# Layer 1's GpSimd subtraction in two halves, and seven VectorE steps of a weight conversion spread over four tiles

## The chip, the cores and the metric

The kernel runs on one core of one Trainium2 chip. The metric is the device time of one execution in microseconds; the time before is the median of three runs. TensorE does the matrix products, VectorE, ScalarE and GpSimd the elementwise work, SyncE (SP) and GpSimd issue transfers.

## The reference

A two-dimensional Fourier transform (real part) of four sequences of 3008 rows and 256 columns, followed by two feed-forward layers over the 12032 rows. The weights are float64.

```python
def reference(x, moe_w_in, moe_w_out, moe2_w_in, moe2_w_out):
    X = np.fft.fft(np.fft.fft(x, axis=1), axis=2).real.astype(np.float32)
    X = X.reshape(4 * 3008, 256)
    h = X @ moe_w_in                      # 256 x 2048
    X = (np.maximum(h, 0.0) ** 2) @ moe_w_out      # 2048 x 256
    h = X @ moe2_w_in
    return ((h * np.cos(h)) @ moe2_w_out).astype(np.float32)
```

## The kernel before

All products are done with operands split into two parts of 12 bits each (a high one, `h`, and a low one, `l`), so that each product is three matmuls: high by high, low by high, high by low. The transform along the rows is done with folded tables, the transform along the columns is multiplied into the first weights.

Layer 1 goes over 12 blocks of up to 512 pairs of tokens (the last has 388), and in each block over 16 tiles of 128 hidden columns: 192 tiles, numbered `i` from 0. A pair holds the sum and the difference of two halves, so that a tile is 128 by 2 by 512. The chain of one tile is:

- `l1_mm1`: TensorE, six matmuls into a PSUM buffer `h`, of which there are two; then `l1_add` on VectorE: `u` (line 450) and the two sums `s` (line 206 in the helper `tt`), which read `h` and so release it for the tile after the next.
- `l1_act` on ScalarE: three instructions of 128x1024, relu, square, and the high part `gh`.
- `l1_lo` on GpSimd (line 470): `gl = s - gh`, 128x1024.
- `l1_mm2`: TensorE, twelve matmuls into `acc`, three tiles later (`LAG`).

After 16 tiles `l1_out` takes `acc` out: two instructions on ScalarE, two of 128x1024 on VectorE (`ol`), stored by SP. Layer 2 follows in the same manner with 128x512 halves.

Each engine executes its instructions in the order in which the program issues them. That order comes from the class `Order`: each piece of work is given a time, in units of one tile, and all are issued in the order of these times. Work of tile `i` has the times `i` (`l1_mm1`), `i + 0.4` (`l1_add`), `i + 0.6`, `i + 0.8` and `i + 3.3`; a table `TIMES` holds other times for much of the work before tile 107, and is the same in both kernels.

The weights come as float64 and are converted by `from_f64` in steps on VectorE, with `size_f64` on ScalarE ahead of them. For layer 1's weights this lies in tiles 0 to 18, with some steps handed to ScalarE and GpSimd (`shared`). For layer 2's weights there are 16 pieces of 128x512, one for every four tiles from 113 on: piece `p` is loaded by SP at time 111 + 4p (`load_cv`), sized on ScalarE at 113 + 4p, and converted by `conv_w2` at 113.5 + 4p: seven VectorE instructions one behind the other (lines 164, 165, 166, 171, 175, 176, 178), then two stores to DRAM. The converted weights are read back from tile 181 on. The folds of batches 1 to 3 (`fold_a`, `fold_eo`, `fold_b`, `fold_lo`) are VectorE work of the same kind, spread over tiles 11 to 24, 36 to 48 and 84 to 96.

Of the kernel before, what the change touches and what calls it, by code (L numbers as in the profile page):

```python
# [10 lines left out]
F32 = mybir.dt.float32  # L11
F32R = mybir.dt.float32r
I32 = mybir.dt.int32
# [29 lines left out]
# the upper half of float64's least value that float32 holds too, read as float32  # L43
SMALLEST = float(np.array([0x38100000], np.int32).view(np.float32)[0])

# columns of the transforms' tables, one for each part
# [6 lines left out]
# of each part of a transform, by columns of the result: (column, width, ((unit of the data, column of the table), ..))  # L53
# [6 lines left out]
# of each tile of rows: (sum over even or over odd places, rows)  # L60
# [3 lines left out]
# the places in the order of issue of instructions that do not have the one they get by rule; what converts with help from other engines; which engine folds  # L64
# [5 lines left out]
class Order:  # L70
    """Instructions gathered with a time each and issued in the order of those times."""
# [13 lines left out]
def f32(ap):  # L85
    return ap.bitcast(F32)
# [3 lines left out]
def kernel(ctx: ExitStack, tc: tile.TileContext, x, x128, cs, tab0, tab1, w_in1, w_out1, w_in2, w_out2, out):  # L90
# [36 lines left out]
    # a chunk of a layer's weights holds four tiles of d_ff, as two parts of 12 bits each  # L127
# [26 lines left out]
    def from_f64(key, st, hi, lo, pool=fft, shared=False):  # L154
        """float64 as the sum of two float32r: the first holds 12 bits, the second the rest, rounded to 12 bits."""
        n = st.shape[1]
        w0, w1 = st[:, :, 0], st[:, :, 1]
        r = w1.bitcast(F32)
        v = nc.vector
        got = {}  # L160

        def upper():
            a = got["a"] = buf("f64t", "f64t", I32, pool, 2, (P, BLK))[:, :n]
            v.tensor_scalar(out=a, in0=w1, scalar1=0x07FFFE00, scalar2=3, op0=ALU.bitwise_and, op1=ALU.logical_shift_left)  # L164
            v.scalar_tensor_tensor(out=a, in0=w1, scalar=-0x40000000, in1=a, op0=ALU.bitwise_and, op1=ALU.bitwise_or)  # L165
            v.tensor_scalar(out=w1, in0=w1, scalar1=0x1FF, scalar2=None, op0=ALU.bitwise_and)
            if shared:
                nc.scalar.activation(r, w1, AF.Copy, scale=2.0 ** -20)
                nc.gpsimd.tensor_tensor(out=r, in0=w0.bitcast(F32), in1=r, op=ALU.add)
            else:  # L170
                v.scalar_tensor_tensor(out=r, in0=w0.bitcast(U32), scalar=2.0 ** -32, in1=w1, op0=ALU.mult, op1=ALU.add)

        def parts():
            a = got["a"]
            v.scalar_tensor_tensor(out=hi, in0=sizes.pop(key), scalar=SMALLEST, in1=a.bitcast(F32), op0=ALU.is_ge, op1=ALU.mult)  # L175
            v.tensor_scalar(out=a, in0=hi.bitcast(I32), scalar1=-0x800000, scalar2=None, op0=ALU.bitwise_and)  # L176
            if not shared:
                v.scalar_tensor_tensor(out=lo, in0=r, scalar=2.0 ** -20, in1=a.bitcast(F32), op0=ALU.mult, op1=ALU.mult)

        def lower():  # L180
            if shared:
                nc.gpsimd.tensor_tensor(out=lo, in0=r, in1=got["a"].bitcast(F32), op=ALU.mult)

        return upper, parts, lower

# [38 lines left out]
    def fold_b(b, t):  # L224
        ra, rb = raws[b, t]
        eo = units(rb, "p (e a d) -> p e a d", e=2, a=4)
        # units: cosE s s', sinO s s', cosO s s', sinE s s'
        f = units(ra, "p (i a b d) -> p i a b d", i=2, a=2, b=2)
        for i, op in enumerate(PM):
            tt(f[:, i], eo[:, :, 0::2], eo[:, :, 1::2], op)  # L230
        # units: eeC, eoS, eoC, eeS
        fv = units(ra, "p (a b d) -> p a b d", a=4, b=2)
        g = units(rb, "p (i a d) -> p i a d", i=4, a=2)
        for i, op in enumerate(PM):
            tt(g[:, i], fv[:, 0:4:3, 0], fv[:, 0:4:3, 1], op)

    def fold_hi(b, t):
        ra, rb = raws[b, t]
        # units: sinO s s', cosO s s', eeC, eoS, eoC, eeS
        src = (units(ra, "p (a n) -> p a n", a=4)[:, 1:3], units(rb, "p (a n) -> p a n", a=4)[:, 0:2])  # L240
        parts = [buf(f"d{p}", f"d{p}", F32R, fft, NT, (P, 2, 2, 2 * P)) for p in "hl"]
        for i in range(2):
            nc.scalar.activation(parts[0][:, i], src[i], AF.Copy)
        raws[b, t] = src, parts
# [11 lines left out]
    def fold_128():  # L256
# [5 lines left out]
        # units: cosO s s', eeC, eoC  # L262
# [28 lines left out]
    def both(s, n, a, m):  # L291
        """The sums over even and over odd places, added and subtracted."""
        for i in (1, 0):
            tt(s[:m, i, :n], s[:m, 0, :n], a[:m, 1, :n], PM[i])
# [94 lines left out]
    def conv_w2(name, c, q):  # L389
        parts = [buf(f"cv{p}", f"cv{p}", F32R, late["pool"], 2, (P, BLK)) for p in "hl"]  # L390
        for fn in from_f64((name, c, q), wst.pop((name, c, q)), *parts, late["pool"]):
            fn()
        for p, dst in zip(parts, w2_dram[name, c]):
            nc.sync.dma_start(out=dst[:, q * BLK:(q + 1) * BLK], in_=f32(p))
# [28 lines left out]
    def direct_z(i, s, hi, lo):  # L423
        """The first block's columns stay on the chip; the rest of the sums s goes to DRAM."""
# [41 lines left out]
    def l1_lo(k, f):  # L466
        w = BLOCKS[k][1]
        hi, s = gs[1, k, f], ss.pop((k, f))
        lo = gl_buf()
        nc.gpsimd.tensor_tensor(out=lo[:, :, :w], in0=s[:, :, :w], in1=f32(hi)[:, :, :w], op=ALU.subtract)  # L470
        gs[1, k, f] = hi, lo
# [129 lines left out]
    def convert(t, key, st, fn, steps=(-0.5, 0, 0, 0)):  # L601
# [3 lines left out]
        def start():  # L605
            got.extend(fn(shared))
            got[0]()

        at(t + steps[0], lambda: size_f64(key, st(), shared=shared), ("size", key))
        for i, f in enumerate((start, lambda: got[1](), lambda: got[2]())):  # L610
            at(t + steps[1 + i], f, ("conv", key, i))
# [96 lines left out]
    for i, job in enumerate((n, c, q) for n in ("in", "out") for c in range(NCH) for q in range(2)):  # L708
        at(111 + 4 * i, lambda job=job: load_cv(*job))
        at(113 + 4 * i, lambda job=job: size_f64(job, wst[job], late["pool"]))  # L710
        at(113.5 + 4 * i, lambda job=job: conv_w2(*job))
# [28 lines left out]
def _order():  # L740
    """The place along s of each row of the folded data, or -1: even ones, odd ones, the last of both."""
# [12 lines left out]
def _tables():  # L754
    """The transforms' cosines and sines, in two parts of 12 bits each."""
# [15 lines left out]
# the places along d, the first half of them; the last row of the sines holds the place in the middle  # L771
# [10 lines left out]
def _rows():  # L782
    """For each of the eight places that fold onto s its row of x, or S where there is none."""
# [9 lines left out]
def _lay_x(x):  # L793
    """x with rows and columns in the order in which they are folded, zeros where nothing folds; the middle column."""
# [16 lines left out]
def _token_columns():  # L811
    """The column of the result in which each token lies."""
# [38 lines left out]
```

## Time and profile before

| | us |
|---|---|
| median of three runs | 2033.5 (2033.21 to 2036.59) |
| span of the profiled execution, first to last instruction | 2030.6 |
| TensorE busy (matmuls) | 1915.8, 94% of the span |
| VectorE busy | 1439.9, 71% |
| ScalarE busy | 1470.2, 72% |
| GpSimd busy | 1043.5, 51% |

The median lies 2.9 us above the span of the profiled execution. The page cuts the span into 40 slices of 50.8 us. From the fifth on TensorE is busy for nine tenths or more, except in three of eight tenths between 711 and 965 us, and from the fourth on its granted clock is at nine tenths or more. In the slices from 608 to 914 us VectorE's share rises to between seven and eight tenths; after about 990 us layer 2 runs, and the slices are alike.

### The profile page before, as it was taken

To read this page: it belongs to the slowest core of one execution; us is meant where nothing else is said; L and a number is where in the kernel's file an instruction comes from. 1 tells how busy PE (TensorE), PEld (TensorE's weight loads), DVE (VectorE), ACT (ScalarE), POOL (GpSimd) and SP (SyncE) were. 2 spreads that over 40 slices of the span, in tenths; PEclk is the share of its full clock that TensorE was granted. 3 is DMA by queue.
4 is the path that set the end of the run, shared out by engine and by line. 5 is a ranking of instruction groups with operands and counts; after the bars stand their busy time and mean duration, and the time that the engine had idled before them with its cause. 6 is when DMAs were issued, how large, how long until landed. Compare 5 with 4: busy or idle time off the path is not lost.

```text
span 2030.6 us, 23279 instructions
## 1 busy us (share of the span) xinstructions
PE 1915.8 (94%) x8544; PEld 1587.5 (78%) x8544; DVE 1439.9 (71%) x1558; ACT 1470.2 (72%) x1519; POOL 1043.5 (51%) x524
## 2 busy tenths in 40 slices
PE   5678999999999988998999999999999999999999
PEld 4466877887787776777888888888888888888899
DVE  8999576457847878887576666666666666666666
ACT  3666777787767767667787777777777777777776
POOL 5455655564555645555554444544444544444443
PEclk8789999999999999999999999999999999999999
DMA  6222231212222233223611111111111111111110
GB/s 245 91 89 83 87 111 69 80 61 90 83 85 101 68 109 104 88 89 113 192 52 32 32 31 32 53 42 32 31 32 32 52 43 31 32 32 32 51 33 16
DMA packets 64389, 140.17 MB, mean 69 GB/s; under 512 B 7680, under 2 KB 19088, under 8 KB 64276
## 3 DMA queue, kind: packets, MB, share of 16 engines
q1 hardware_dynamic: 41524, 89.20, 12.4%
q0 software_dynamic: 22752, 49.49, 8.4%
q8 instruction: 67, 1.10, 0.2%
q14 instruction: 46, 0.38, 0.1%
HBM read 81.98 MB, written 56.69 MB: 68 GB/s over the span
## 4 chain that ended last, share of the span: by engine, by line
PE 75%; DVE 18%; issue 2%; ACT 2%; DMA 2%; POOL 1%; DVEq 0%; ACTq 0%; POOLq 0%; SPq 0%
PE acc L566 25%; PE h L515 17%; PE acc L482 15%; PE h L443 8%; PE acc L515 8%; DVE s L206 4%; DVE u L450 2%; DVE f64t L165 2%; PE h L281 2%; DVE inB L206 2%; DVE cvh L175 1%; DVE f64t L164 1%; DVE f64t L176 1%; DVE inA L206 1%; DMA ol<-ol 1%
## 5 line engine op out<-in xcount | busy, mean ns | idle before, releaser
L554 POOL TENSOR_TENSOR gl<-r,gh 128x1024 fp32r<-128x1024 f32 (+1 forms) x189 | 446.2, 2361 | 540.0 <-ACT gh L547 465.9
L470 POOL TENSOR_TENSOR gl<-s,gh 128x1024 fp32r<-128x1024 f32 (+1 forms) x192 | 466.5, 2430 | 353.1 <-ACT gh L463 311.3
L460 ACT ACTIVATE s<-s 128x1024 f32<-128x1024 f32 (+1 forms) x192 | 199.1, 1037 | 196.0 <-DVE s L206 188.6
L529 DVE SCALAR_TENSOR_TENSOR r<-n,h 128x1024 f32<-128x1024 int32 (+1 forms) x129 | 154.7, 1199 | 214.6 <-ACT n L521 214.6
L450 DVE SCALAR_TENSOR_TENSOR u<-zb,wc,h 128x512 f32<-128x512 f32 (+1 forms) x192 | 141.0, 734 | 178.9 <-PE h L443 174.4
L206 DVE TENSOR_TENSOR s<-u,h 128x512 f32<-128x512 f32 (+1 forms) x384 | 242.7, 674 | 24.5 <-POOL inB L319 2.6
L521 ACT ACTIVATE n<-h 128x1024 int32<-128x1024 f32 (+1 forms) x129 | 130.4, 1011 | 155.3 <-PE h L515 155.3
L482 PE MATMUL acc<-gh,wbh 128*128 128x512 f32 (+1 forms) x768 | 242.3, 398 | 0.0
L482 PE MATMUL acc<-gh,wbl 128*128 128x512 f32 (+1 forms) x768 | 238.8, 393 | 0.0
L482 PE MATMUL acc<-gl,wbh 128*128 128x512 f32 (+1 forms) x768 | 237.6, 391 | 0.0
L529 DVE SCALAR_TENSOR_TENSOR r<-n,r 128x1024 f32<-128x1024 int32 (+1 forms) x192 | 232.7, 1212 | 6.6
L443 PE MATMUL h<-xh,wah 128*128 128x512 f32 (+3 forms) x384 | 159.2, 415 | 71.8 <-DVE s L206 63.7
L537 ACT ACTIVATE r<-r,halfpi 128x1024 f32<-128x1024 f32 (+1 forms) x192 | 218.3, 1137 | 6.2
L461 ACT ACTIVATE s<-s 128x1024 f32<-128x1024 f32 (+1 forms) x192 | 200.5, 1044 | 6.1
L463 ACT ACTIVATE gh<-s 128x1024 fp32r<-128x1024 f32 (+1 forms) x192 | 200.5, 1044 | 6.1
L536 ACT ACTIVATE r<-r 128x1024 f32<-128x1024 f32 (+1 forms) x192 | 198.3, 1033 | 6.7 <-DVE r L529 6.7
L566 PE MATMUL acc<-gh,wbl 128*128 128x512 f32 (+1 forms) x768 | 202.2, 385 | 0.0
L566 PE MATMUL acc<-gh,wbh 128*128 128x512 f32 (+1 forms) x768 | 202.1, 385 | 0.0
L566 PE MATMUL acc<-gl,wbh 128*128 128x512 f32 (+1 forms) x768 | 202.1, 385 | 0.0
L515 PE MATMUL h<-xh,wah 128*128 128x512 f32 (+1 forms) x516 | 199.0, 386 | 3.0 <-issue 1.5
L515 PE MATMUL h<-xh,wal 128*128 128x512 f32 (+1 forms) x516 | 198.8, 385 | 0.0
L515 PE MATMUL h<-xl,wah 128*128 128x512 f32 (+1 forms) x516 | 198.8, 385 | 0.0
(160 smaller groups left out, 3513.9 us busy)
## 6 DMA issues: line engine op xcount, KB each, us to landing
oh<-oh SPq DMA_DIRECT2D x22, 512.0 KB, 2.9
ol<-ol SPq DMA_DIRECT2D x22, 512.0 KB, 2.7
xh<-oh POOLq DMA_DIRECT2D x22, 512.0 KB, 3.9
xl<-ol POOLq DMA_DIRECT2D x22, 512.0 KB, 5.0
y_out<-o SPq DMA_DIRECT2D x44, 256.0 KB, 3.9
inA<-x_in SPq DMA_DIRECT2D x12, 512.0 KB, 3.9
inB<-x_in SPq DMA_DIRECT2D x10, 512.0 KB, 5.9
xh<-zh POOLq DMA_DIRECT2D x10, 512.0 KB, 4.1
```

What stands on the lines that cost most here:

```text
L206: nc.vector.tensor_tensor(out=out, in0=in0, in1=in1, op=op)
L443: nc.tensor.matmul(a[:, i, :w], st, mv[:m, i, :w], start=j == 0, stop=j == 2)
L460: nc.scalar.activation(s[:, :, :w], s[:, :, :w], AF.Relu)
L461: nc.scalar.activation(s[:, :, :w], s[:, :, :w], AF.Square)
L463: nc.scalar.activation(hi[:, :, :w], s[:, :, :w], AF.Copy)
L470: nc.gpsimd.tensor_tensor(out=lo[:, :, :w], in0=s[:, :, :w], in1=f32(hi)[:, :, :w], op=ALU.subtract)
L482: nc.tensor.matmul(accs[1, k][m][:, n, :w], wt, g[:, n, :w], start=f == 0 and i == 0, stop=f == NF - 1 and i == 2)
L515: nc.tensor.matmul(a[:, j, :w], st, mv[:, m, :w], start=m == 0 and q == 0, stop=m == 1 and q == 2)
L529: nc.vector.scalar_tensor_tensor(out=r[:, :, :w], in0=n[:, :, :w], scalar=-c, in1=src[:, :, :w], op0=ALU.mult, op1=ALU.add)
L537: nc.scalar.activation(r[:, :, :w], r[:, :, :w], AF.Sin, bias=halfpi, scale=-1.0)
L554: e.tensor_tensor(out=lo[:, :, :w], in0=r[:, :, :w], in1=f32(hi)[:, :, :w], op=ALU.subtract)
L566: nc.tensor.matmul(accs[2, k][:, m, :w], w_out_t([c[part] for c in wo2], f, m), g[:, j, :w], start=f == 0 and q == 0, stop=f == NF - 1 and ...
```

## The change

Two edits. `l1_lo` subtracts in two instructions of 128x512 in place of one of 128x1024. And `from_f64` returns seven functions of one VectorE step each in place of three; `convert`, which serves layer 1's weights, calls them in the groups that stood there before, and `conv_w2` gives them times of their own, 4/7 of a tile apart, with the stores at 3.9 tiles behind the first step. The other lines of the difference are comments that fell away.

```diff
     def from_f64(key, st, hi, lo, pool=fft, shared=False):
...
-        def upper():
+        def mask():
             a = got["a"] = buf("f64t", "f64t", I32, pool, 2, (P, BLK))[:, :n]
             v.tensor_scalar(out=a, in0=w1, scalar1=0x07FFFE00, scalar2=3, op0=ALU.bitwise_and, op1=ALU.logical_shift_left)
-            v.scalar_tensor_tensor(out=a, in0=w1, scalar=-0x40000000, in1=a, op0=ALU.bitwise_and, op1=ALU.bitwise_or)
+
+        def merge():
+            v.scalar_tensor_tensor(out=got["a"], in0=w1, scalar=-0x40000000, in1=got["a"], op0=ALU.bitwise_and, op1=ALU.bitwise_or)
+
+        def rest():
             v.tensor_scalar(out=w1, in0=w1, scalar1=0x1FF, scalar2=None, op0=ALU.bitwise_and)
+
+        def join():
             if shared:
...
-        def parts():
+        def upper_part():
...
+        def power():
...
-        def lower():
+        def lower_part():
...
-        return upper, parts, lower
+        return mask, merge, rest, join, upper_part, power, lower_part
...
-    def conv_w2(name, c, q):
-        parts = [buf(f"cv{p}", f"cv{p}", F32R, late["pool"], 2, (P, BLK)) for p in "hl"]
-        for fn in from_f64((name, c, q), wst.pop((name, c, q)), *parts, late["pool"]):
-            fn()
-        for p, dst in zip(parts, w2_dram[name, c]):
-            nc.sync.dma_start(out=dst[:, q * BLK:(q + 1) * BLK], in_=f32(p))
+    def conv_w2(t, name, c, q):
+
+        got = {}
+
+        def begin():
+            got["p"] = [buf(f"cv{p}", f"cv{p}", F32R, late["pool"], 2, (P, BLK)) for p in "hl"]
+            got["f"] = from_f64((name, c, q), wst.pop((name, c, q)), *got["p"], late["pool"])
+
+        def store():
+            for p, dst in zip(got["p"], w2_dram[name, c]):
+                nc.sync.dma_start(out=dst[:, q * BLK:(q + 1) * BLK], in_=f32(p))
+
+        at(t, begin)
+        for j in range(7):
+            at(t + 4 / 7 * j, lambda j=j: got["f"][j]())
+        at(t + 3.9, store)
...
         lo = gl_buf()
-        nc.gpsimd.tensor_tensor(out=lo[:, :, :w], in0=s[:, :, :w], in1=f32(hi)[:, :, :w], op=ALU.subtract)
+        for n in range(2):
+            nc.gpsimd.tensor_tensor(out=lo[:, n, :w], in0=s[:, n, :w], in1=f32(hi)[:, n, :w], op=ALU.subtract)
...
-        at(113.5 + 4 * i, lambda job=job: conv_w2(*job))
+        conv_w2(113.5 + 4 * i, *job)
```

VectorE's row at the second piece, of the kernel before. `u` and `s` are a tile's additions, `f` is the loaded piece, `f64t`, `cvh` and `cvl` are the conversion's results:

```order
L450 SCALAR_TENSOR_TENSOR u_4956<-zb,wc_96,h 128x512
L206 TENSOR_TENSOR s<-u_4956,h 128x512 x2
L164 TENSOR_SCALAR f64t<-f_4878 128x512
L165 SCALAR_TENSOR_TENSOR f64t<-f_4878,f64t 128x512
L166 TENSOR_SCALAR f_4878<-f_4878 128x512
L171 SCALAR_TENSOR_TENSOR f_4878<-f_4878 128x512
L175 SCALAR_TENSOR_TENSOR cvh<-size,f64t 128x512
L176 TENSOR_SCALAR f64t<-cvh 128x512
L178 SCALAR_TENSOR_TENSOR cvl<-f_4878,f64t 128x512
L450 SCALAR_TENSOR_TENSOR u_4998<-zb,wc_96,h 128x512
L206 TENSOR_TENSOR s<-u_4998,h 128x512 x2
```

VectorE's row at the same piece, of the kernel after; its lines 469 and 215 are 450 and 206 of before, and 164 to 190 the seven steps:

```order
L215 TENSOR_TENSOR s<-u_5071,h 128x512 x2
L164 TENSOR_SCALAR f64t<-f_4987 128x512
L167 SCALAR_TENSOR_TENSOR f64t<-f_4987,f64t 128x512
L469 SCALAR_TENSOR_TENSOR u_5109<-zb,wc_96,h 128x512
L215 TENSOR_TENSOR s<-u_5109,h 128x512 x2
L170 TENSOR_SCALAR f_4987<-f_4987 128x512
L177 SCALAR_TENSOR_TENSOR f_4987<-f_4987 128x512
L469 SCALAR_TENSOR_TENSOR u_5144<-zb,wc_96,h 128x512
L215 TENSOR_TENSOR s<-u_5144,h 128x512 x2
L180 SCALAR_TENSOR_TENSOR cvh<-size,f64t 128x512
L183 TENSOR_SCALAR f64t<-cvh 128x512
L469 SCALAR_TENSOR_TENSOR u_5177<-zb,wc_96,h 128x512
```

Seven steps between two tiles' additions became two, two, two and one, the last behind the fourth tile's additions; the next piece begins one tile later in the same way.

GpSimd's row early in layer 1, before and then after (`gl` is the subtraction, `inB` and `wo` are steps of layer 1's weights):

```order
L470 TENSOR_TENSOR gl<-s,gh 128x1024
L319 TENSOR_TENSOR zl<-z,zh 128x2x378
L470 TENSOR_TENSOR gl<-s,gh 128x1024
L169 TENSOR_TENSOR inB_488<-inB_488 128x512
L470 TENSOR_TENSOR gl<-s,gh 128x1024
```

```order
L490 TENSOR_TENSOR gl<-s,gh 128x512 x2
L328 TENSOR_TENSOR zl<-z,zh 128x2x378
L490 TENSOR_TENSOR gl<-s,gh 128x512 x2
L175 TENSOR_TENSOR inB_489<-inB_489 128x512
L490 TENSOR_TENSOR gl<-s,gh 128x512 x2
```

Each subtraction is now two instructions in the same place, and nothing else on GpSimd moved. On SP a piece's two stores moved behind the load of the next piece, and where a block ends behind the four stores of its results; the orders of TensorE and ScalarE are unchanged.

## Rows read from the trace of the kernel before

**Rows 1.** Busy time by stage, microseconds; the first line names the columns.

```profile
core 0: us, PE busy (x) PEld busy (x) DVE busy (x) ACT busy (x) POOL busy (x), PEclk, DMA share, GB/s
42.60:250.00 207.40, 170.42 (x746) 134.33 (x745) 177.03 (x226) 137.90 (x156) 117.32 (x62) 0.89 0.28 91
250.00:440.00 190.00, 184.49 (x832) 151.22 (x832) 121.02 (x162) 141.43 (x144) 109.17 (x49) 0.97 0.24 82
...
480.00:550.00 70.00, 64.27 (x265) 51.75 (x264) 61.33 (x72) 50.22 (x51) 38.55 (x17) 0.95 0.23 77
...
621.02:937.70 316.68, 278.28 (x1136) 223.47 (x1134) 260.50 (x306) 209.62 (x210) 163.59 (x71) 0.94 0.28 94
```

**Rows 2.** That last stage, first product (L443) alone, six matmuls a tile.

```profile
621.02:937.70 316.68, 105.68 (x379) 73.65 (x378) 0.94 0.28 94
```

**Rows 3.** Waits in 621 to 938 us: total, times, longest.

```profile
PE h L443 <- DVE s L206: 38.4, 14, 4.5
```

**Rows 4.** TensorE in order of time: start, us, instruction, [idle before].

```profile
621.02 0.39 PE L443 MATMUL h<-xh,wah 128*128 128x512 f32 x1
...
625.12 0.39 PE L443 MATMUL h<-xh,wah 128*128 128x512 f32 x1
...
695.73 0.50 PE L443 MATMUL h<-xh,wah 128*128 128x512 f32 x1 [1.81 <-DVE s L206]
...
698.05 1.06 PE L482 MATMUL acc<-gh,wbl 128*128 128x512 f32 x2
...
701.12 0.62 PE L482 MATMUL acc<-gl,wbh 128*128 128x512 f32 x2
```

**Rows 5.** Groups of VectorE's steps in 621 to 938 us, by line.

```profile
...
L166 DVE TENSOR_SCALAR f<-f 128x512 int32<-128x512 int32 x16 | 14.7, 920 | 1.9 <-ACT size L150 0.5
L171 DVE SCALAR_TENSOR_TENSOR f<-f 128x512 f32<-128x512 uint32 x16 | 13.2, 823 | 0.6
...
L206 DVE TENSOR_TENSOR ol<-acc,oh 128x1024 fp32r<-128x1024 f32 x8 | 9.4, 1216 | 0.0
```

**Rows 6.** VectorE's instructions on tile f64t: five of the seven steps.

```profile
621.02:937.70 316.68, 101.95 (x80) 0.00 (x0) 0.94 0.28 94
```

**Rows 7.** VectorE in order of time, sixth piece: first and last step.

```profile
728.89 0.47 DVE L164 TENSOR_SCALAR f64t<-f 128x512 int32<-128x512 int32 x1
...
733.05 0.74 DVE L450 SCALAR_TENSOR_TENSOR u<-zb,wc,h 128x512 f32<-128x512 f32 x1
```

**Rows 8.** VectorE in order of time, fourth piece and the tile behind it.

```profile
...
685.09 0.47 DVE L164 TENSOR_SCALAR f64t<-f 128x512 int32<-128x512 int32 x1
685.59 2.78 DVE L165 SCALAR_TENSOR_TENSOR f64t<-f,f64t 128x512 int32<-128x512 int32 x1
...
689.55 2.89 DVE L175 SCALAR_TENSOR_TENSOR cvh<-size,f64t 128x512 fp32r<-128x512 bf16 x1
...
693.54 0.74 DVE L450 SCALAR_TENSOR_TENSOR u<-zb,wc,h 128x512 f32<-128x512 f32 x1
694.39 1.29 DVE L206 TENSOR_TENSOR s<-u,h 128x512 f32<-128x512 f32 x2
```

**Rows 9.** GpSimd in order of time, around the fourth piece.

```profile
...
682.84 4.98 POOL L470 TENSOR_TENSOR gl<-s,gh 128x1024 fp32r<-128x1024 f32 x2
689.01 2.88 POOL L470 TENSOR_TENSOR gl<-s,gh 128x1024 fp32r<-128x1024 f32 x1 [1.19 <-DVE f L166]
...
```

**Rows 10.** VectorE's additions of tile 113.

```profile
623.45 1.28 DVE L206 TENSOR_TENSOR s<-u,h 128x512 f32<-128x512 f32 x2
```

**Rows 11.** GpSimd beside that addition.

```profile
624.11 2.41 POOL L470 TENSOR_TENSOR gl<-s,gh 128x1024 fp32r<-128x1024 f32 x1 [1.41 <-ACT gh L463]
```

**Rows 12.** All engines, tile 117: from VectorE's sums to GpSimd's subtraction.

```profile
645.87 1.29 DVE L206 TENSOR_TENSOR s<-u,h 128x512 f32<-128x512 f32 x2
...
650.64 2.65 POOL L470 TENSOR_TENSOR gl<-s,gh 128x1024 fp32r<-128x1024 f32 x1 [2.48 <-ACT gh L463]
```

**Rows 13.** Instructions on tile f64t: duration ns min/median/max, first and last start.

```profile
...
L182 POOL TENSOR_TENSOR wbl<-wo,f64t x7: 1290/1327/2159, 82.1 to 165.6; 128x512 fp32r<-128x512 f32 x7
...
```

More of the change, by code (lines that the diff above doesn't have):

```diff
@@ L171, in upper @@
                 v.scalar_tensor_tensor(out=r, in0=w0.bitcast(U32), scalar=2.0 ** -32, in1=w1, op0=ALU.mult, op1=ALU.add)
-        def parts():
[L174 to L178, printed above, removed]
-        def lower():
+        def upper_part():
+            v.scalar_tensor_tensor(out=hi, in0=sizes.pop(key), scalar=SMALLEST, in1=got["a"].bitcast(F32), op0=ALU.is_ge, op1=ALU.mult)
+        def power():
+            v.tensor_scalar(out=got["a"], in0=hi.bitcast(I32), scalar1=-0x800000, scalar2=None, op0=ALU.bitwise_and)
+        def lower_part():
+            a = got["a"].bitcast(F32)
             if shared:
-                nc.gpsimd.tensor_tensor(out=lo, in0=r, in1=got["a"].bitcast(F32), op=ALU.mult)
-        return upper, parts, lower
+                nc.gpsimd.tensor_tensor(out=lo, in0=r, in1=a, op=ALU.mult)
+            else:
+                v.scalar_tensor_tensor(out=lo, in0=r, scalar=2.0 ** -20, in1=a, op0=ALU.mult, op1=ALU.mult)
+        return mask, merge, rest, join, upper_part, power, lower_part
     raws, dat, jobs = {}, {}, {}
@@ L606, in start, with middle, last @@
             got.extend(fn(shared))
-            got[0]()
+            for g in got[:4]:
+                g()
+        def middle():
+            for g in got[4:6]:
+                g()
+            if not shared:
+                got[6]()
+        def last():
+            if shared:
+                got[6]()
         at(t + steps[0], lambda: size_f64(key, st(), shared=shared), ("size", key))
-        for i, f in enumerate((start, lambda: got[1](), lambda: got[2]())):
+        for i, f in enumerate((start, middle, last)):
             at(t + steps[1 + i], f, ("conv", key, i))
```

## The prediction

> **What bounds the kernel now.** I read the page's 40 slices first: TensorE is busy nearly throughout, but between 609 and 914 us its share and its granted clock dip while VectorE's share rises. Then the busy time by stage [rows 1]. From tile 113's first product at 621.02 us to tile 176's at 937.70 lie 63 tiles (378 weight loads by six a tile, [rows 2]) in 316.68 us. Undisturbed, one tile follows the other after 4.10 us (625.12 - 621.02, [rows 4]), so 63 tiles want 258.3 us: this stage loses 58.4 us. Two views account for it. TensorE is idle for 316.68 - 278.28 = 38.4 us, all of it waiting for VectorE's sums `s` [rows 1, 3]; and its granted clock is 0.94 on average, so that 0.06 x 316.68 = 19.0 us of cycles are missing. The clock is at its full level (2.4 GHz) before such a wait and at half of it (1.2 GHz) behind the longer ones: behind the wait that ends at 695.73, pairs of matmuls take 1.06 us, and 0.62 once the clock is back [rows 4]. The rest of the losses stand in the stages of the first weights and of the folds, where VectorE is nearly full or TensorE idles beside it [rows 1].
>
> Why `s` is late: the seven steps of a piece stand in one burst between two tiles' additions. Undisturbed, the burst takes 733.05 - 728.89 = 4.16 us [rows 7]. On average it takes (101.95 + 14.7 + 13.2) / 16 = 8.1 us [rows 5, 6]; the other 3.9 us are waits inside instructions. The fourth piece shows what for: GpSimd runs two subtractions back to back from 682.84, 4.98 us together. Line 164's step comes at 685.09, just as the first ends, and takes 0.47; line 165's comes at 685.59 and lasts 2.78 instead of some 0.69, until 688.37, which is 0.55 behind GpSimd's second end at 687.82 [rows 8, 9]. So a step and a subtraction take turns: whichever has begun keeps the other out to its end, and a step that waits gets in between two subtractions. The additions, which read PSUM, show no such wait.
>
> The burst is too long for the cover it has. Tile 113's sums end at 623.45 + 1.28 = 624.73 [rows 10]; TensorE wants that buffer for tile 115, at 621.02 + 8.20 = 629.22. VectorE may be 4.5 us late; a burst of 8.1 us less the idle VectorE had (4.10 - 2.24 = 1.9 a tile) is later than that.
>
> **The change part by part.** *The seven steps, spread.* Nothing is removed: 16 x 4.16 us of steps stay on VectorE. Additions take 0.74 + 1.29 and 0.11 between, so 2.14, or 2.24 from one to the next (rows 8: 693.54, 694.39). Four tiles of these (9.0), a piece (4.2) and a quarter of a block's two `ol` (9.4 / 16 = 0.6, [rows 5]) make 13.7 us of the 16.4 that TensorE needs for four tiles. That leaves 2.7 us for waits, and 4.5 us of lateness that may build up and be paid back.
>
> How long the waits are I walk through by hand. Time 0 is the end of the additions after which a piece begins. GpSimd starts 3.5 us behind the end of the sums it works on (645.87 + 1.29 to 650.64, [rows 12]; ScalarE's three instructions lie between). With tiles 4.10 apart, the previous tile's subtraction has started at -0.6, which is where 624.11 lies against 624.73 [rows 11]. A half of it: no row shows this form; 2.41 / 2 = 1.21 is the bound below, and 1.33, the median of another GpSimd operation of 128x512 with two inputs, the bound above [rows 13]. I take 1.26, between them, and 0.08 between two (4.98 - 2 x 2.41 over two, rounded up).
> - First tile: the first half ends at 0.6, the first step gets in and ends at 0.9; the second half ends at 2.1, the second step at 2.6. The additions end at 4.7, where 4.1 would be punctual: 0.6 late.
> - Second: the previous subtraction started at 3.5 and ends at 6.1; both steps are done by 7.1, the additions end at 9.2, 1.0 late.
> - Third: GpSimd starts at 8.2, the first half ends at 9.5; the step that waits ends at 10.0, the second half at 11.3, the next step at 11.6; the additions end at 13.7, 1.4 late.
> - Fourth, one step: the first half ends at 13.9, the step at 14.5, the additions at 16.6, 0.2 late. By now the next subtraction starts at 17.2, so the next piece's first two steps run free (16.6 to 17.8) and the additions are punctual again.
>
> The lateness stays at 1.4 us; with a block's two `ol` in the same tile (2 x 1.2 us more) at 3.8, still under 4.5. By this walk TensorE waits no more and its clock has no reason to fall. The margin is thin in the tiles where a block ends, and the walk is sensitive to a few tenths, so I leave 8 us of the 58.4 (half a microsecond a piece) and count 50 gained. What is late next is TensorE itself, at 4.10 us a tile.
>
> *The halves.* GpSimd does 192 x about 0.2 us more (2 x 1.26 + 0.08 - 2.41). It hides in GpSimd's idle time, since it is then busy for 2.6 of 4.1 us a tile, and `gl` is used three tiles later. Were that cover gone, it would cost 0.2 us a tile. In return a VectorE step with such a wait waits for at most one half. That matters also ahead of tile 113, in the first weights and the folds. There, from 250 to 440 and from 480 to 550 us, TensorE idles for 5.5 + 5.7 us and lacks 0.03 x 190 + 0.05 x 70 = 9.2 us of clock, and from 43 to 250 us VectorE is busy for 177 of 207 us [rows 1]. Where several steps stand in a row, the second half catches the next one, so little is saved. Bounds: -18 us (most of that 20) and +5 (GpSimd's 0.2 in each of some 25 tiles of the first stage). I take -5, nearer to nothing than to the end.
>
> *The rest.* SP's stores come later, each behind a wait for the last step; behind them in SP's queue stands the load of the next piece but one, whose first reader is two tiles (8.2 us) off, and the stored weights are read from tile 181 on, four tiles after the last store. I count nothing; had a load to wait for the store, ScalarE's size instruction would hold up its chain by as much. `convert` issues the same order as before.
>
> Sum, against the profiled execution's span: 2030.6 - 50 - 5 = 1975.6 us. The median lies 2.9 us above that span, so 1978.5.
>
> **A rule that speaks against it.** The rows show a step kept out to the end of a subtraction, and one subtraction held up by a step (2.88 us at 689.01 for 2.41, [rows 9]). The Trainium skill, SBUF — State Buffer, section "Who interferes with whom", says the same of the port pair that VectorE shares with GpSimd: an exclusive lock, held for a whole instruction, and taken also by a VectorE instruction with two inputs in SBUF. By that rule all seven steps are of the kind that waits, and the trace agrees (line 164 and line 165 both wait). It would make spreading a cost, since each step asks anew; that is the third rival below.
>
> **The rivals.**
> 1. *VectorE becomes the bound.* If a step does not get in between the two halves, the walk changes: the steps wait for the whole subtraction, 2.6 us, and only the fourth tile pays back. Additions then end at 5.1, 9.2, 14.3 and 18.0: 1.6 us late for each piece, plus 0.6 for `ol`; 16 x 2.2 less the 4.5 us of cover, which is there once, leaves 31 of the 58 us lost, and the halves bring nothing elsewhere: 2033.5 - 27 = 2006. For it: the gap between two subtractions is short. Against it: at 685.09 a step did get in. Chance 0.22.
> 2. *The halves do more than I count.* The folds and the first weights lose most of their waits: 18 us in place of 5, and the whole 58 us here: 2033.5 - 58 - 15 = 1960. For it: VectorE is the late engine there too. Against it: the steps stand in rows there. Chance 0.10.
> 3. *Slower: each step meets a half.* Seven waits of 1.26 us make 8.8 in place of 3.9, and a piece of four tiles 13.7 + 8.8 = 22.5 us of VectorE against the 316.68 x 4 / 63 = 20.1 of now: 16 x 2.4 = 38 us more, 2072. It decides from 6.4 us of waits a piece on (20.1 - 13.7), 0.9 a step. For it: GpSimd and VectorE's free time fall together in each tile. Against it: the walk finds 0.4 to 0.9 for the waiting ones, and some run free. Chance 0.05.
> 4. *Nothing to measure.* The change does what it says on VectorE, but TensorE's waits return elsewhere in the same sum, for instance on `gl`, whose subtraction now ends later: 2033. Against it: rows 3 and the cover of three tiles. Chance 0.03.
>
> **How the numbers follow.** Forecast 0.60, rivals 0.22, 0.10, 0.05, 0.03. The time is 1978. The range goes from 1960 (rival 2) to 2010 (rival 1 with the bound of +5): it leaves out rivals 3 and 4 and the outer parts of 1 and 2, some 0.17. Faster by over 0.2% (4 us, about what a measurement of this kernel can tell from no change): 0.92; within it 0.03; slower 0.05.
>
> **What would show it.** Right: from tile 113 to tile 176 some 266 us in place of 316.7, with a granted clock of 0.99 or more and under 10 us of TensorE's first product waiting for `s`; 384 subtractions of about 1.26 us; steps of a piece that last at most 1.3 us longer than their 0.4 to 0.7. Wrong: steps of 2 to 3 us still (the halves run as one), first products that wait a little in most tiles (rival 1), or ends of blocks with waits over 2 us, at which the clock falls to half again.

## The result and the profile after

The changed kernel takes 1971.7 us (median of four runs, 1970.0 to 1974.1) against 2033.4: 0.969 of the time before, with an interval of 0.968 to 0.971. The profiled execution's span fell from 2030.6 to 1968.2 us, by 62.4. It splits by TensorE's first products as before:

| | before | after | gain |
|---|---|---|---|
| start to tile 113's first product | 621.02 us | 614.32 us | 6.7 |
| tile 113's to tile 176's (63 tiles) | 316.68 | 259.65 | 57.0 |
| from there to the end | 1092.9 | 1094.2 | -1.3 |

The slices of the page: the dip of TensorE and of its clock around 609 to 914 us is gone, and VectorE's row reads nine where it read seven and eight.

```profile
PE   5688999999999999999999999999999999999999
...
DVE  8999587455947999995766666666666666666666
...
PEclk9789999999999999999999999999999999999999
```

Busy time by stage, as [rows 1]; the last line is the 63 tiles:

```profile
core 0: us, PE busy (x) PEld busy (x) DVE busy (x) ACT busy (x) POOL busy (x), PEclk, DMA share, GB/s
41.62:248.86 207.24, 174.20 (x747) 136.96 (x746) 176.95 (x228) 137.91 (x156) 128.38 (x94) 0.89 0.29 92
248.86:614.32 365.46, 355.52 (x1627) 291.83 (x1626) 235.52 (x318) 276.74 (x279) 234.01 (x179) 0.99 0.25 83
614.32:873.97 259.65, 259.10 (x1136) 212.87 (x1134) 246.75 (x303) 213.28 (x212) 182.23 (x134) 1.00 0.35 113
```

TensorE is now busy for 259.10 of 259.65 us with the clock at its full level; 63 tiles at 4.10 us are 258.3. VectorE is busy for 246.75 of them: it is nearly full, and does not hold TensorE up. The waits of that stage, where 38.4 us stood before [rows 3]:

```profile
...
DVE u L469 <- PE h L462: 1.9, 1, 1.9
...
PE h L462 <- DVE s L215: 0.3, 1, 0.3
...
```

TensorE's wait for `s` is 0.3 us in all. But the other line says as much: VectorE waited once, for 1.9 us, for a first product. In all other tiles it came to its additions after the product was there. So it is late all through the stage, and stays within the cover. What the stage still takes over 258.3 us lies where a block ends (tiles 132, 163 and 164, against the same tiles of a run without any loss, the quarters below).

VectorE in order of time, the sixth piece (164, 167, 170, 177, 180, 183 and 190 are the seven steps, 469 and 215 the additions):

```profile
...
702.39 0.42 DVE L164 TENSOR_SCALAR f64t<-f 128x512 int32<-128x512 int32 x1
702.85 0.69 DVE L167 SCALAR_TENSOR_TENSOR f64t<-f,f64t 128x512 int32<-128x512 int32 x1
703.46 0.74 DVE L469 SCALAR_TENSOR_TENSOR u<-zb,wc,h 128x512 f32<-128x512 f32 x1
704.33 1.29 DVE L215 TENSOR_TENSOR s<-u,h 128x512 f32<-128x512 f32 x2
705.53 0.72 DVE L170 TENSOR_SCALAR f<-f 128x512 int32<-128x512 int32 x1
706.29 0.69 DVE L177 SCALAR_TENSOR_TENSOR f<-f 128x512 f32<-128x512 uint32 x1
...
708.95 1.03 DVE L180 SCALAR_TENSOR_TENSOR cvh<-size,f64t 128x512 fp32r<-128x512 bf16 x1
710.01 1.57 DVE L183 TENSOR_SCALAR f64t<-cvh 128x512 int32<-128x512 int32 x1
...
713.58 1.41 DVE L190 SCALAR_TENSOR_TENSOR cvl<-f,f64t 128x512 fp32r<-128x512 f32 x1
...
```

GpSimd beside it, two halves a row:

```profile
...
703.15 2.82 POOL L490 TENSOR_TENSOR gl<-s,gh 128x512 fp32r<-128x512 f32 x2 [1.60 <-ACT gh L482]
706.87 2.56 POOL L490 TENSOR_TENSOR gl<-s,gh 128x512 fp32r<-128x512 f32 x2 [0.90 <-ACT gh L482]
710.01 2.74 POOL L490 TENSOR_TENSOR gl<-s,gh 128x512 fp32r<-128x512 f32 x2 [0.57 <-DVE cvh L180]
713.14 3.01 POOL L490 TENSOR_TENSOR gl<-s,gh 128x512 fp32r<-128x512 f32 x2 [0.40 <-PE acc L502]
...
```

The steps at 702.39 and 702.85 run free, others wait for one half: 708.95 lasts 1.03 us for 0.69, 710.01 lasts 1.57 for 0.43, 713.58 lasts 1.41 for 0.69. None lasts 2.8 us, as in [rows 8]; the longest of the stage lasts 1.82. This piece is one of the cheapest, 6.5 us of steps for 7.9 on average. The step of line 167, which runs free here, waits in the other fifteen:

```profile
...
L167 DVE SCALAR_TENSOR_TENSOR f64t<-f,f64t 128x512 int32<-128x512 int32 x16 | 26.1, 1634 | 0.5
...
```

Of the 112 steps 71 wait for more than 0.1 us, each for one half. One half takes 1.3 us in the middle (min, median and max in ns):

```profile
...
L490 POOL TENSOR_TENSOR gl<-s,gh x384: 1012/1299/2282, 52.8 to 932.2; 128x512 fp32r<-128x512 f32 x176, 128x388 fp32r<-128x388 f32 x16
...
```

### The profile page after: what moved, and what is told of

The parts are those of the page before. It is cut to its first block, busy times and chain, and to the rows that moved or that the text cites. A ratio compares the mean times of both kernels' runs of the same rounds, so it can differ in the third digit from the quotient of the medians.

```text
span 1968.2 us, 23258 instructions
## 1 busy us (share of the span) xinstructions
PE 1896.0 (96%) x8544; PEld 1575.4 (80%) x8544; DVE 1424.7 (72%) x1558; ACT 1472.3 (75%) x1519; POOL 1093.3 (56%) x716
## 4 chain that ended last, share of the span: by engine, by line
PE 66%; DVE 11%; ACT 4%; issue 2%; DMA 0%; DVEq 0%; POOL 0%; ACTq 0%
PE acc L586 26%; PE h L535 17%; PE acc L502 9%; PE acc L535 8%; PE h L462 4%; DVE s L215 4%; DVE u L469 2%; ACT s L480 1%; ACT s L479 1%; DVE cvh L180 1%; DVE f L177 1%; PE h L290 1%; DVE f L170 1%; DVE ol L215 1%; ACT gh L482 1%
## 5 line engine op out<-in xcount | busy, mean ns | idle before, releaser
L490 POOL TENSOR_TENSOR gl<-s,gh 128x512 fp32r<-128x512 f32 (+1 forms) x384 | 515.8, 1365 | 247.8 <-ACT gh L482 213.5
L567 ACT ACTIVATE gh<-r 128x1024 fp32r<-128x1024 f32 (+1 forms) x192 | 197.1, 1027 | 0.3 <-DVE r L215 0.3
```

The lines of the kernel that those rows point to most:

```text
L490: nc.gpsimd.tensor_tensor(out=lo[:, n, :w], in0=s[:, n, :w], in1=f32(hi)[:, n, :w], op=ALU.subtract)
```

## The experiments

All numbers of stages are from tile 113's first product to tile 176's, unless it is said otherwise. Four tiles with a piece want 16.4 us; by "steps a piece" I mean the mean times of the seven VectorE instructions, waits and all, added up. It was 8.1 us before and is 7.9 after.

**One part at a time.** The halves with the burst of before, and the spread steps with whole subtractions:

```diff
-            at(t + 4 / 7 * j, lambda j=j: got["f"][j]())
-        at(t + 3.9, store)
+            at(t, lambda j=j: got["f"][j]())
+        at(t, store)
```

> The subtraction in halves as in the kernel after, the seven steps of a piece in one burst as before. Theory (turns): a VectorE step and a GpSimd subtraction keep each other out for a whole instruction, and the loss between tiles 113 and 176 comes from a burst made longer than 4.5 us by these waits. In a burst the second half only catches the next step, so the burst stays near 7 to 8 us and 45 to 58 us of the 58.4 stay lost; ahead of tile 113 the 6.7 us of the kernel after are gained: 2015 to 2027 us. Rival (the halves do it): the waits in a burst are halved from 3.9 to 2 us, the burst is 6.2 us, most of the loss goes: under 2000 us.

Measured: 2025.7 us (0.996 of before, 0.995 to 0.998). Busy time of the stage, columns as above:

```profile
614.04:929.42 315.38, 279.02 (x1135) 223.95 (x1133) 255.57 (x306) 209.82 (x210) 176.52 (x134) 0.94 0.28 94
```

315.38 us for 316.68: in a burst the halves bring nothing to this stage, and the clock stays at 0.94. Ahead of it, tile 113 starts at 614.04, where it starts in the kernel after. The theory's reading holds, the rival falls. But not every wait is the one that it describes. In four of the 16 pieces the first step waits through three or four halves that run back to back:

```profile
...
675.34 4.80 DVE L164 TENSOR_SCALAR f64t<-f 128x512 int32<-128x512 int32 x1
...
```

```profile
...
674.78 5.07 POOL L490 TENSOR_TENSOR gl<-s,gh 128x512 fp32r<-128x512 f32 x4
...
```

So a step that waits does not always get in between two subtractions, as the prediction has it. Why it does in most places and not here, no run shows.

```diff
-        for n in range(2):
-            nc.gpsimd.tensor_tensor(out=lo[:, n, :w], in0=s[:, n, :w], in1=f32(hi)[:, n, :w], op=ALU.subtract)
+        nc.gpsimd.tensor_tensor(out=lo[:, :, :w], in0=s[:, :, :w], in1=f32(hi)[:, :, :w], op=ALU.subtract)
```

> The seven steps spread as in the kernel after, the subtraction whole as before. Theory as in the prediction's first rival: no step gets in between two halves, so two steps a tile wait for whole subtractions, VectorE becomes the bound, and some 31 us of the 58 stay lost between tiles 113 and 176; ahead of them the 6.7 us are lost again: about 2008 us (1998 to 2015). Rival (spreading alone does it): no loss in the stage, 1971.7 + 6.7 = 1978 us (1975 to 1983).

Measured: 1995.2 us (0.981, 0.979 to 0.983), between the two. The stage, and its waits:

```profile
619.17:896.79 277.62, 266.31 (x1136) 215.22 (x1134) 266.97 (x302) 213.56 (x211) 157.61 (x71) 0.98 0.33 105
```

```profile
...
PE h L462 <- DVE s L215: 11.2, 8, 3.2
...
DVE u L469 <- PE h L462: 2.6, 2, 2.0
```

VectorE is busy for 267 of 277.6 us and TensorE waits for it again: VectorE sets the pace, above all where a block ends: 14 of the 19 us lost lie in tiles 131, 132, 147, 148, 163 and 164. Steps a piece are 9.2 us, more than in the burst (8.1), as a whole subtraction is met more often: 59 of the 112 steps wait, for 35 in the burst. Spreading alone gets back 39 of the 57 us, the halves alone 1, both together 57: the halves pay in this stage only once the steps are spread. The first rival of the prediction is this kernel's state; its price was 31 us lost, a little in every piece, measured are 277.6 - 258.3 = 19.3, most of it at three ends of blocks.

**Is it the subtraction that the steps wait for?** The kernel before, with GpSimd's subtraction left out in tiles 112 to 177:

```diff
     def l1_lo(k, f):
         w = BLOCKS[k][1]
         hi, s = gs[1, k, f], ss.pop((k, f))
+        if 7 <= k < 11 or k == 11 and f < 2:
+            gs[1, k, f] = hi, hi
+            return
         lo = gl_buf()
```

> As the kernel before (burst, whole subtractions), but in tiles 112 to 177 GpSimd's subtraction is left out and the low part's product reads the high part, so the output there lacks the low part. VectorE's steps then meet no GpSimd instruction. Theory (turns): the burst is 4.2 us as in the sixth piece, less 1.9 us of idle time is within the cover of 4.5 us; the stage takes 258 to 263 us in place of 316.7 with the clock at its full level: 1975 to 1982 us. Rival (the burst as such is too long, whatever GpSimd does): the stage stays above 290 us, over 2005 us.

Measured: 1974.2 us (0.970, 0.969 to 0.972). The stage:

```profile
617.48:877.58 260.10, 259.52 (x1136) 212.77 (x1135) 197.38 (x309) 213.25 (x213) 7.35 (x9) 1.00 0.35 114
```

With nothing on GpSimd to meet, the seven steps take 4.0 us and the burst 4.12, in every one of the 16 pieces, and the stage takes 260.1 us with the clock at its full level, burst or not. So the loss of before is neither the steps' work nor their lying together: it is their waits for the subtraction, added to a burst that has cover for so much and no more.

How much cover, can be read from the bursts one by one: from the start of the first step to the start of the next additions, and what lies beyond 16.4 us between the first product of the tile behind the piece's first and that of four tiles later. Pieces where a block ends, and the last one, are left out, and of like ones one stands. (The four with a block's end lose 6.0 to 7.3 us each in the kernel before, 26.6 of its 58.4 us: the two `ol` come on top of the burst there.)

| kernel | burst, us | lost, us |
|---|---|---|
| without the subtraction | 4.12 (all) | 0.0 |
| before | 4.16, 6.55 | 0.0, 0.2 |
| before | 7.15, 8.38, 9.17 | 0.8, 2.0, 2.8 |
| before | 8.45, 9.16, 10.10 | 3.8, 4.4, 5.2 |
| halves, burst | 7.10, 7.86 | 0.8, 1.5 |
| halves, burst | 8.96, 10.42 | 4.3, 5.7 |
| quarters, burst (below) | 5.75, 6.70, 7.58, 8.41 | 0.0, 0.4, 1.2, 2.1 |

Nothing is lost up to 6.4 us, which is the 4.5 us that VectorE may be late and the 1.9 us that it is idle in a tile; beyond that each microsecond costs one, and in the five bursts that lost 3.8 us or more, 1.5 to 1.7 us on top. In these, and in none of the others, TensorE's clock fell to half behind the wait, as behind the fourth piece of before (8.45, [rows 4]): six to eight matmuls there start 0.43 us apart in place of 0.23.

**Fewer tiles, more work.** A piece in two tiles, two tiles without any; and one step four times, which adds three steps to each piece:

```diff
-            at(t + 4 / 7 * j, lambda j=j: got["f"][j]())
-        at(t + 3.9, store)
+            at(t + 2 / 7 * j, lambda j=j: got["f"][j]())
+        at(t + 1.95, store)
```

> As the kernel after, but a piece's seven steps lie within two tiles (2/7 of a tile apart) and two tiles follow without any. Four steps and then three: 2.2 us and 1.8 us of steps, some 2.5 and 1.5 us of waits, less 1.9 us of idle time in each tile: VectorE is 2.8 and then 4.2 us late, just under the 4.5 us of cover, and pays it back in the two free tiles. Theory: little or no loss, 1972 to 1985 us. Rival (only two steps a tile fit): a loss of 1 to 2 us a piece, 1988 to 2004 us.

Measured: 1977.8 us (0.972, 0.971 to 0.974). The stage:

```profile
615.32:882.58 267.26, 262.74 (x1136) 215.10 (x1134) 239.54 (x306) 212.36 (x212) 174.73 (x134) 0.99 0.33 110
```

A loss of 9.0 us against 258.3, half of it idle time of TensorE (267.26 - 262.74). It is no loss of each piece: 8.9 of it lie at the four ends of blocks (tiles 115 and 116, 131 and 132, 147 and 148, 163 and 164), where `ol` comes on top of a lateness that just stays under the cover elsewhere.

```diff
-            v.tensor_scalar(out=got["a"], in0=hi.bitcast(I32), scalar1=-0x800000, scalar2=None, op0=ALU.bitwise_and)
+            for _ in range(1 if pool is fft else 4):
+                v.tensor_scalar(out=got["a"], in0=hi.bitcast(I32), scalar1=-0x800000, scalar2=None, op0=ALU.bitwise_and)
```

> As the kernel after, but the step of line 183 runs four times in each of layer 2's pieces (the same result each time): three more steps of 0.43 us and what they wait. It measures how much room VectorE has. By the sum of the prediction, 13.7 us of work in 16.4 become 15.1, and 1.3 us are left for waits of some 3 to 4 us: if VectorE is that near to being the bound, each piece loses up to 2 us, 1976 to 2004 us. Rival (the waits shrink as VectorE gets later, since the steps then fall where GpSimd is idle): no loss, 1971 to 1975 us.

Measured: 1993.0 us (0.980, 0.978 to 0.981). The stage, and in 614 to 896 us the group of the repeated step (busy, mean ns):

```profile
614.91:896.26 281.35, 266.86 (x1136) 213.97 (x1135) 261.72 (x352) 212.11 (x213) 177.95 (x134) 0.99 0.32 104
```

```profile
...
L184 DVE TENSOR_SCALAR f64t<-cvh 128x512 int32<-128x512 int32 x60 | 64.4, 1073 | 2.1
...
```

The stage takes 21.7 us longer than in the kernel after. 48 steps were added; each takes 1.07 us with its waits for 0.43 alone, 51 us in all, of which 30 found room or took the place of other steps' waits. So the changed kernel stands near the edge. VectorE is not busy for some 13 us of its stage (259.65 - 246.75), but little of that is room: where it sets the pace, with the steps spread and whole subtractions, 10.7 us remain too (277.62 - 266.97), most of them short gaps between instructions. Beyond that it has what its waits give up when it gets later, and then it is the bound.

**Smaller pieces of the subtraction.** Four instructions of 128x256, then eight of 128x128:

```diff
         for n in range(2):
-            nc.gpsimd.tensor_tensor(out=lo[:, n, :w], in0=s[:, n, :w], in1=f32(hi)[:, n, :w], op=ALU.subtract)
+            for q in (slice(0, w // 2), slice(w // 2, w)):
+                nc.gpsimd.tensor_tensor(out=lo[:, n, q], in0=s[:, n, q], in1=f32(hi)[:, n, q], op=ALU.subtract)
```

> As the kernel after, with the subtraction in four instructions of 128x256. Theory: a GpSimd instruction costs its columns and about 0.1 us, so a tile's subtraction is 2.8 us in place of 2.6 and still hidden; the stage from tile 113 to 176 has nothing left to gain (259.65 us for 258.3); ahead of it waits are a little shorter: 1968 to 1974 us. Rival (a fixed cost of 0.4 us or more an instruction): GpSimd is busy for over 4.1 us a tile and sets the pace, over 1990 us.

Measured: 1961.7 us (0.964, 0.963 to 0.966), 10 us under the kernel after and better than I expected. The stage has no loss at all, and VectorE's busy time in it falls by 33 us; steps a piece are 5.3 us for 7.9:

```profile
608.38:866.68 258.30, 258.30 (x1135) 213.12 (x1134) 213.94 (x307) 216.41 (x214) 217.02 (x261) 1.00 0.34 113
```

The two stages ahead of it took 207.24 and 365.46 us in the kernel after:

```profile
41.78:243.98 202.20, 169.16 (x746) 133.40 (x745) 172.39 (x228) 138.12 (x156) 145.04 (x157) 0.92 0.29 94
243.98:608.38 364.40, 356.20 (x1627) 291.54 (x1626) 233.06 (x318) 276.82 (x279) 265.77 (x339) 0.99 0.25 83
```

The first is 5.0 us shorter, in which VectorE is nearly full with the first weights. This is more than the traces scatter: it takes 207.2 to 209.8 us in the eight kernels with whole subtractions or halves, and 202.2 to 204.4 in the four with quarters. GpSimd pays for it: one tile's subtraction without VectorE's steps beside it takes 2.41 us whole [rows 11], and in the kernels with halves, quarters and eighths:

```profile
559.79 2.55 POOL L490 TENSOR_TENSOR gl<-s,gh 128x512 fp32r<-128x512 f32 x2 [3.01 <-ACT gh L482]
...
```

```profile
...
568.64 2.84 POOL L491 TENSOR_TENSOR gl<-s,gh 128x256 fp32r<-128x256 f32 x4 [2.46 <-ACT gh L482]
...
```

```profile
...
573.10 3.38 POOL L491 TENSOR_TENSOR gl<-s,gh 128x128 fp32r<-128x128 f32 x8 [1.37 <-ACT gh L482]
...
```

2.55, 2.84 and 3.38 us: about 0.14 us for each further instruction.

```diff
-            for q in (slice(0, w // 2), slice(w // 2, w)):
+            for q in (slice(i * w // 4, (i + 1) * w // 4) for i in range(4)):
```

> As the kernel after, with the subtraction in eight instructions of 128x128. Quarters took 2.83 us a tile on GpSimd and halves 2.55, so each further instruction costs 0.14 us: 3.4 us a tile, still under 4.1. Theory: the stage stays at 258 us, and ahead of tile 113 waits get shorter once more, by less than the 6 us from halves to quarters: 1956 to 1963 us. Rival (GpSimd's own work becomes late, its other steps for the first weights above all): over 1965 us.

Measured: 1979.6 us (0.973, 0.970 to 0.976; its runs lie apart, 1971.4 to 1987.8), slower than quarters. The profiled span is 20.5 us longer than with quarters (1979.7 for 1959.2). Of these 11.6 lie in the stage, 4.7 ahead of it and 4.2 behind it:

```profile
613.07:882.99 269.92, 261.56 (x1135) 212.00 (x1133) 231.86 (x302) 212.50 (x210) 251.41 (x514) 1.00 0.33 108
```

GpSimd is busy for 251.4 of 269.9 us, its waits for VectorE included, and its own work has become late. In the waits of 40 to 608 us, columns as above, VectorE and TensorE wait for `gl`; with quarters the same two lines say 4.0 and 2.8 us in all, and in the kernel before VectorE waited for 1.8 us in the whole run:

```profile
...
DVE s L215 <- POOL gl L491: 15.7, 16, 2.5
PEld acc L503 <- POOL gl L491: 12.9, 15, 1.8
...
```

The rival's mechanism, then, but it is not alone. Two steps of the stage are kept out by subtractions that run back to back, 19 of 128x128 in the first case and 23 in the second:

```profile
...
667.05 8.01 DVE L164 TENSOR_SCALAR f64t<-f 128x512 int32<-128x512 int32 x1
...
```

```profile
...
870.59 9.55 DVE L164 TENSOR_SCALAR f64t<-f 128x512 int32<-128x512 int32 x1
...
```

Behind them come the largest losses of the stage, 2.4 us in tile 127 and 3.8 in tile 175. So a finer grain does not bound a step's wait by one instruction: as in the burst with halves, a queue of subtractions can pass a step as a whole. Of the numbers of instructions tried, four are best.

Quarters with the burst of before:

```diff
-            at(t + 4 / 7 * j, lambda j=j: got["f"][j]())
-        at(t + 3.9, store)
+            at(t, lambda j=j: got["f"][j]())
+        at(t, store)
```

> The subtraction in four instructions of 128x256, the seven steps of a piece in one burst as in the kernel before. Theory (the loss is what a burst is longer than VectorE's cover of 4.5 us and an idle 1.9): steps and quarters take turns, so a burst of 4.2 us meets four waits of at most 0.65 us, 6.8 us in all and 4.9 us late: it just oversteps the cover, by less than in halves. The stage from tile 113 to 176 takes 259 to 280 us, 1962 to 1983 us in all. Rival (only spreading helps, as halves in a burst brought nothing there): the stage takes 310 us or more, over 2010 us.

Measured: 1992.4 us (0.979, 0.977 to 0.980). One burst of it, first and last step and the additions behind them, and the stage:

```profile
...
647.67 0.46 DVE L164 TENSOR_SCALAR f64t<-f 128x512 int32<-128x512 int32 x1
648.16 1.11 DVE L167 SCALAR_TENSOR_TENSOR f64t<-f,f64t 128x512 int32<-128x512 int32 x1
...
653.38 1.11 DVE L190 SCALAR_TENSOR_TENSOR cvl<-f,f64t 128x512 fp32r<-128x512 f32 x1
654.41 0.74 DVE L469 SCALAR_TENSOR_TENSOR u<-zb,wc,h 128x512 f32<-128x512 f32 x1
...
```

```profile
606.60:894.79 288.19, 266.25 (x1136) 213.81 (x1134) 243.67 (x306) 209.33 (x210) 216.70 (x259) 0.99 0.32 103
```

The burst is 6.74 us here, as I had worked out, but they run from 5.7 to 8.4, and I had taken all for alike: the stage takes 288 us and not 280 at most. The table above has the pieces. Quarters without spreading get back half of the loss.

Quarters, spread, with the added steps of above:

```diff
+            for _ in range(1 if pool is fft else 4):
+                v.tensor_scalar(out=got["a"], in0=hi.bitcast(I32), scalar1=-0x800000, scalar2=None, op0=ALU.bitwise_and)
```

> Quarters and spread steps, with the step of line 183 four times in each of layer 2's pieces. With halves these 48 extra steps cost 21 us. With quarters VectorE was busy for 214 of 258 us in the stage, where it was busy for 247 of 260 with halves. Theory (the room comes from shorter waits): no loss in the stage, 1960 to 1965 us. Rival (VectorE's share is not what decides): again some 20 us, about 1982 us.

Measured: 1974.1 us (0.970, 0.969 to 0.972), between the theory and its rival. The stage:

```profile
609.20:877.91 268.71, 262.10 (x1135) 211.30 (x1134) 251.76 (x350) 211.04 (x212) 210.13 (x257) 1.00 0.34 109
```

The added steps cost 10.4 us here for 21.7 with halves; they wait less (0.79 us each, 47.5 over 60), but VectorE is full again at 252 of 268.7 us, and 7.1 of the 10.4 us lie at the ends of blocks.

**Two versions that were to be better.**

On top of quarters (one of three places shown, the others likewise):

```diff
-                nc.gpsimd.tensor_tensor(out=lo, in0=r, in1=a, op=ALU.mult)
+                for q in (slice(0, n // 2), slice(n // 2, n)):
+                    nc.gpsimd.tensor_tensor(out=lo[:, q], in0=r[:, q], in1=a[:, q], op=ALU.mult)
```

> Quarters and spread steps, and GpSimd's other long instructions ahead of tile 113 (the two steps for the first weights, and the subtraction behind each transform) in pieces of at most 256 columns too. Theory (VectorE, nearly full until 200 us, waits for whatever GpSimd runs): a few microseconds more, 1955 to 1961 us. Rival (the cost of more instructions delays the weights' low parts, for which TensorE waits there): no change or slower, 1961 to 1967 us.

Measured: 1961.2 us (0.964, 0.962 to 0.965), the same as quarters: the two steps for the first weights and the subtraction behind the transforms don't matter. With quarters it is the fastest of the kernels run, 0.5% under the changed one (1961.7 / 1971.7).

The folds of batches 2 and 3, each VectorE instruction with a place of its own (cut to its core; `fold_eo`, `fold_b` and `fold_lo` take the index of the instruction):

```diff
+            if b > 1:
+                for j, (fn, i) in enumerate(((fold_a, ()), (fold_eo, (0,)), (fold_eo, (1,)), (fold_b, (0,)), (fold_b, (1,)), (fold_b, (2,)),
+                                             (fold_b, (3,)), (fold_hi, ()), (fold_lo, (0,)), (fold_lo, (1,)))):
+                    at(t0 + 4 / 9 * j, lambda b=b, t=t, fn=fn, i=i: fn(b, t, *(() if not i else (nc.vector, i) if fn is fold_lo else (i,))))
+                continue
```

> As the kernel after, with the same cure for the folds of batches 2 and 3: their nine VectorE instructions a fold get places of their own, 4/9 of a tile apart, and the loads come 1.95 tiles ahead of them. In the kernel after TensorE still lacks some 6 us of idle time and 4 us of clock around the folds of batch 2, and 5 us around those of batch 3. Theory: most of that comes back, 1960 to 1967 us. Rival (the folds' loads and the stores of a block's results stand in each other's way on SP, or the data come late): no change or slower, 1970 to 1980 us.

Measured: 1972.2 us (0.969, 0.968 to 0.971), no change. From tile 34 to tile 113:

```profile
249.44:615.14 365.70, 356.00 (x1628) 291.35 (x1626) 240.60 (x318) 276.26 (x279) 237.32 (x179) 0.99 0.25 83
```

365.70 us for 365.46 in the kernel after, with as much idle time of TensorE (9.7 us for 9.9). Nearly all of it is waits for VectorE's sums in both: 9.8 us before layer 1's products in the kernel after, here 8.0 there and 1.6 before a transform's product, which also waits for VectorE. In the kernel after they lie in tiles 44, 49, 89, 93 and 95, here in tiles 40, 48, 49, 87, 92, 94, 95 and 99. So VectorE is late in other tiles, by as much in all; why the spreading that helps behind tile 113 doesn't help here stays open.

## Why the prediction was right

It said 1978 us (1960 to 2010); it is 1971.7. By its own steps:

- **The loss of 58.4 us and its cause.** Right. The stage now takes 1.4 us more than 63 x 4.10, and the run without subtractions shows that the waits for GpSimd are what made the burst too long. The cover of 4.5 us and the 1.9 us of idle time show in the bursts one by one.
- **The walk by hand.** Its waits are right in size, its end is not. It summed to 3.9 us of waits in the first piece (16.6 - 4 x 2.14 - 4.16); measured are 7.9 - 4.0 = 3.9 a piece. That is about as much as in the burst (8.1 - 4.0 = 4.1): the change hardly shortened the waits, it gave each a cover of its own. The sum ahead of the walk left only 2.7 us for them, and yet they fit. Its 13.7 us were too high: without the subtraction VectorE is busy for 197.4 us in the 63 tiles, 12.5 for four. But the walk let VectorE be punctual again by the next piece. In the trace it is late nearly always, and line 167's step, the second of a piece, which the walk has run free, waits in 15 of 16 pieces. What keeps TensorE from waiting is the cover, and the margin is as thin as the text feared: with three steps more a piece, or with whole subtractions, VectorE is the bound.
- **8 us left for irregular pieces.** Too much: 1.4 us. This is the largest part of the difference. They lie where the prediction saw the thin margin, at the ends of blocks, and so do 8.9 of the 9.0 us lost with a piece in two tiles and 14 of the 19 with whole subtractions.
- **The halves ahead of tile 113: 5 us.** 6.7 by these two traces. But three kernels whose order is the same up to tile 112 (before, spread only, without subtractions) reach tile 113 at 621.0, 619.2 and 617.5 us, so a single pair of traces is uncertain by 2 or 3; the four kernels with halves there come to 614.0 to 615.3. The means differ by 4.6.
- **0.2 us a tile for two instructions, hidden.** Right: 0.14, and TensorE waits 0.2 us for `gl` in the whole run.
- **The rivals.** The first (VectorE becomes the bound) is, in its milder form, what the spread alone does. It did not come about with halves, since all 71 steps that wait in the stage wait for one half alone. The prediction took this turn-taking for a rule; the burst with halves and the eighths show that it isn't one, and that the spread steps always got their turn is in part luck. The second (the halves do more than I count) came true by half: 57 of the 58.4 us came back here, but 6.7 and not 18 ahead of tile 113. Its time has a slip, 15 where it says 18; with 18 it would be some 1957. The third would have needed 6.4 us of waits a piece; the most that any run shows is 9.2 - 4.0 = 5.2, with whole subtractions. The Trainium skill, SBUF — State Buffer, section "Who interferes with whom", states that the lock is held for a whole instruction. The runs agree: bursts take 4.12 us without a subtraction, and the longest step of the spread kernels lasts 2.80 us with whole subtractions, 1.82 with halves and 1.24 with quarters. The 9.55 us with eighths are many such instructions in a row.

## What to carry to other kernels

Where two engines keep each other out for whole instructions, the length of the shared instruction and the place of the other engine's steps belong together: short instructions cost 0.14 us each here and pay most when the steps between them are spread: in a burst halves brought 1 us of the 58 and quarters half of it. An engine may be late by what its consumers can bear plus its idle time; a burst under that costs nothing, and the excess is what one pays, so it helps to spread work even if the sum of the waits stays the same. A wait of this kind stands inside the instruction's duration (2.8 us for 0.7) and not in the idle time before it: look for instructions whose durations vary.

## What was not expected of the hardware

A subtraction in quarters made the whole kernel 10 us faster than in halves, while VectorE's steps fell from 7.9 to 5.3 us a piece; I had taken the gain for exhausted with halves. And eight pieces were worse again, at 3.4 us a tile of GpSimd's 4.1. Nor was it expected that a step of 0.42 us could be kept out for 9.55 us by a row of short instructions, each of which takes 0.46 alone.
